# A linear-attention and channel-mix kernel on one core: a new written-out table of instruction order, the last tile's two parts exchanged, and one vector loaded by one DMA

## The chip, the core and the metric

The kernel runs on one core of a Trainium2 chip. The metric is the device time in microseconds of one launch. The five engines go by their short names: PE (TensorE, the matmuls; PEld is the loading of its weights), ACT (ScalarE), DVE (VectorE), POOL (GpSimd, which here does little beyond issuing the casting loads) and SP (SyncE, which issues the stores and the DMA transposes).

## The reference, cut to what matters

There are 8 batches, 8 heads, 576 tokens, a head dimension of 64, a model width of 512 and a hidden width of 1024.

```python
kv  = np.einsum('bhsd,bhse->bhde', k, v)            # 64 x 64 for each head
out = np.einsum('bhsd,bhde->bhse', q, kv)
x   = out / sqrt(mean(out * out) + 1e-6) * g_norm   # norm over each head's 64 values
# x is then (batch, token, 512); x_prev is x moved down by one token
xk = mu_k * x + (1 - mu_k) * x_prev
xr = mu_r * x + (1 - mu_r) * x_prev
k  = np.maximum(xk @ w_k, 0.0)
v  = k * k @ w_v
return sigmoid(xr @ w_r) * v
```

## The kernel before

All tiles are allotted by hand and the order of all work is written out by hand too: `ORDER` (L18 to L109) is a table of eight strings, and the loop at L806 goes through its words from left to right and calls one small function for each. A word such as `K.2.4.0=7` is an operation's name, its arguments, and the PSUM banks that it takes; a quote mark at the end gives the operation to DVE, otherwise to ACT (where there is a choice). Every engine runs its own instructions in the table's order, and waits only for the data, the banks and the buffers that it needs. Nothing reorders at run time, so an instruction that waits holds up all that stands behind it on its engine.

The words that the text speaks of, with b the batch:

- `ld.n.b` (L195) is a load of batch b that casts to bf16, issued by POOL; n is 0 for k, 1 for v, 2 for q. Tiles are shared: for even b from 2 on, k goes to `sq0`, v to `qT0` and q to `q0`; for odd b they have tiles of their own (`in_k`, `in_v`, `in_q`). Before it issues, POOL does a small copy (`passed`, L194) for each DMA transpose that the table has issued since the last load, and so waits until that transpose has landed.
- `qd.b` (L302) is a DMA transpose of q, issued by SP, for b from 3 on. `yd.b` (L410) is one of the normalised y into `xT`, for b from 4 on. Both stand in SP's queue between the stores of the output.
- `kv.b` (L287, 72 small matmuls) makes k'v. `kvo` and `kvs` copy it out of PSUM and swap its halves. `u.b.part` (L317, 72 small matmuls over the three parts) makes q times that. `sq`, `red`, `nw`, `mul` square, sum, take the root and multiply; for b under 4, `x` and `x0` (L437) turn the result on PE, and `xo`, `x0o` move it to `xT`. For b from 4 on `yd` turns it, and `gx.b.h` multiplies by g_norm in place.
- `wrap.b`, `dif.b`, `sc.b.w.hp` (L603 on ACT, L605 on DVE) and `add.b.w.h` (L620) make xk (w = 0) and xr (w = 1).
- `K.b.fc.h` (L633, four matmuls, for the first batches `Kp`, `Ka`, `Kz`) is one piece of xk @ w_k with its relu (L625 on ACT, L627 on DVE), and `ks.b.fc` (`ksp`) the square (L639 on ACT, L641 on DVE).
- `R.b.t` (L665, four matmuls) is xr @ w_r for 128 tokens with its sigmoid (L668, ACT). `V.b.t.part` (L675, four matmuls each, or `Vq`) is the product with w_v. `fin.b.t` (L688) multiplies the two on DVE and issues two stores from SP; `fip` issues one from SP and `sta` the other one from ACT.
- `L.0` and `L.1` are the last tile of 128 tokens, in two parts of 384 and 128 columns (`last_vv`, L678): eight matmuls each, a multiplication on DVE, and a store from SP and one from ACT.
- `wm` is a number of matmuls on zeros that keep PE busy in the start; `cols` turns the small vectors (mu_k, mu_r, g_norm) into columns.

The eight strings are stages of the pipeline: the third is that of the matmuls K.2, the fourth of K.3, and so on to the eighth with K.7, with the loads and the attention of later batches woven in. PE runs in-order through all of it.

## Time and profile before

| what | value |
|---|---|
| median of the 3 runs (lowest to highest) | 199.93 us (199.44 to 201.73) |
| time of the profiled execution | 199.34 us |
| its span, first to last instruction | 197.5 us |
| granted TensorE clock over the span | 0.994 |
| PE, DVE, ACT, POOL busy | 185.3, 160.5, 131.5, 28.9 us |
| DMA | 32.75 MB, mean 166 GB/s |

The time of the profiled execution is 1.84 us more than its span. PE is busy for 94% of the span. The part of the span in which PE is idle, 12.2 us, is in four places: the wait for the first inputs, short waits all along, one of 1.24 us at 70.87 us, and the last 4.3 us, when the last products are multiplied and stored. A row of a group gives the count of instructions, their busy time and mean duration, and the idle time of the engine just before them with what ended it.

### The profile page before, as it was taken

To read this page: it belongs to the slowest core of one execution; us is meant where nothing else is said; L and a number is where in the kernel's file an instruction comes from. 1 tells how busy PE (TensorE), PEld (TensorE's weight loads), DVE (VectorE), ACT (ScalarE), POOL (GpSimd) and SP (SyncE) were. 2 spreads that over 40 slices of the span, in tenths; PEclk is the share of its full clock that TensorE was granted. 3 is DMA by queue.
4 is the path that set the end of the run, shared out by engine and by line. 5 is a ranking of instruction groups with operands and counts; after the bars stand their busy time and mean duration, and the time that the engine had idled before them with its cause. 6 is when DMAs were issued, how large, how long until landed. Compare 5 with 4: busy or idle time off the path is not lost.

```text
span 197.5 us, 5653 instructions
## 1 busy us (share of the span) xinstructions
PE 185.3 (94%) x2314; PEld 110.0 (56%) x2337; DVE 160.5 (81%) x351; ACT 131.5 (67%) x277; POOL 28.9 (15%) x50
## 2 busy tenths in 40 slices
PE   7699899999999979999999999999999999999991
PEld 2345664565554746567644577665545766654450
DVE  1369989699989987899989998999999695585531
ACT  3465997766947959978784489889835685612420
POOL 7854333020003200113003003000000000000000
PEclk9999999999999999999999999999999999999997
DMA  6999999999999999999999998884916422022865
GB/s 218 214 211 205 194 206 211 204 208 238 189 198 236 161 245 179 240 183 273 195 164 162 165 176 167 177 168 85 176 42 133 110 53 53 0 51 59 186 166 128
DMA packets 42958, 32.75 MB, mean 166 GB/s; under 512 B 23852, under 2 KB 37428, under 8 KB 42932
## 3 DMA queue, kind: packets, MB, share of 16 engines
q0 software_dynamic: 14400, 16.19, 50.7%
q1 hardware_dynamic: 28132, 15.67, 38.3%
q10 hardware_dynamic: 400, 0.52, 1.1%
q8 instruction: 18, 0.29, 0.6%
q14 instruction: 8, 0.07, 0.1%
HBM read 33.56 MB, written 9.44 MB: 218 GB/s over the span
## 4 chain that ended last, share of the span: by engine, by line
PE 76%; DMA 14%; DVE 4%; issue 2%; ACT 1%; POOL 1%; DVEq 0%; POOLq 0%
PE ps_km L633 30%; PE ps_v L675 25%; PE ps_r L665 14%; DMA in_v<-in_v_dram 6%; DMA xT<-yd 4%; DMA q<-in_q_dram 3%; PE ps_u L317 2%; PE ps_kv L287 2%; DVE yd L400 1%; PE ps_x L437 1%; PE ps_v L683 1%; ACT sq__3051 L358 1%; DVE xk__2503 L620 1%; DVE dx__2403 L597 1%; PE ps_qt L331 1%
## 5 line engine op out<-in xcount | busy, mean ns | idle before, releaser
L675 PE MATMUL ps_v<-wv_sb,sqk 128*128 128x512 bf16 x263 | 63.3, 379 | 1.4 <-issue 0.9
L633 PEld LDWEIGHTS <-wk_sb 128*128 128x128 bf16 x480 | 45.7, 98 | 18.3 <-issue 2.0
L675 PEld LDWEIGHTS <-sqk 128*128 128x128 bf16 x280 | 26.5, 98 | 28.6 <-ACT sqk L639 0.2
L665 PE MATMUL ps_r<-wr_sb,xr 128*128 128x512 bf16 x139 | 34.6, 379 | 0.6 <-ACT sq__3051 L358 0.3
L665 PEld LDWEIGHTS <-xr 128*128 128x128 bf16 x144 | 13.9, 98 | 15.3 <-DVE xr L620 0.8
L625 ACT ACTIVATE rt<-ps_km 128x384 bf16<-128x384 f32 (+2 forms) x19 | 9.0, 492 | 3.0 <-PE ps_km L633 1.6
L633 PE MATMUL ps_km<-xk__1455,wk_sb 128*128 128x288 bf16 x64 | 8.8, 286 | 1.2 <-issue 1.2
L633 PE MATMUL ps_km<-xk__2841,wk_sb 128*128 128x288 bf16 x64 | 9.0, 286 | 0.1
L633 PE MATMUL ps_km<-xk__869,wk_sb 128*128 128x192 bf16 (+1 forms) x64 | 8.9, 287 | 0.0
L633 PE MATMUL ps_km<-xk__3378,wk_sb 128*128 128x288 bf16 x64 | 8.8, 286 | 0.0
L633 PE MATMUL ps_km<-xk__2503,wk_sb 128*128 128x288 bf16 x64 | 8.5, 286 | 0.1
L633 PE MATMUL ps_km<-xk__1965,wk_sb 128*128 128x288 bf16 x64 | 8.4, 286 | 0.0
L633 PE MATMUL ps_km<-xk__3218,wk_sb 128*128 128x288 bf16 x64 | 8.3, 286 | 0.0
L260 PE MATMUL ps_warm<-zeros 128*128 128x512 bf16 x21 | 7.2, 464 | 1.2 <-DVE eps L223 1.2
L427 ACT ACTIVATE xT<-xT,cols 128x1152 bf16<-128x1152 bf16 x5 | 6.0, 1245 | 0.5 <-DMA xT<-yd 0.5
L724 PE MATMUL ps_km<-xk__373,wk_sb 128*128 128x320 bf16 x32 | 5.5, 299 | 0.5 <-ACT rs L510 0.4
L427 ACT ACTIVATE xT<-ps_x,cols 128x256 bf16<-128x256 bf16 (+3 forms) x12 | 5.0, 469 | 0.6 <-PE ps_x L437 0.5
L429 DVE TENSOR_SCALAR xT<-ps_x,cols 128x1024 bf16<-128x1024 bf16 (+3 forms) x8 | 3.6, 466 | 1.6 <-PE ps_x L437 1.6
L260 PEld LDWEIGHTS <-zeros 128*128 128x128 bf16 x22 | 2.3, 114 | 4.5 <-issue 2.2
L641 DVE TENSOR_TENSOR sqk<-rt 128x1280 bf16<-128x1280 bf16 (+3 forms) x6 | 4.4, 727 | 0.1
L194 POOL COPY passed<-xT 1x2 bf16<-1x2 bf16 x2 | 0.6, 319 | 26.1 <-DMA xT<-yd 26.1
L724 PEld LDWEIGHTS <-wk_sb 128*128 128x128 bf16 x32 | 2.9, 97 | 2.4 <-issue 1.2
(405 smaller groups left out, 365.4 us busy)
## 6 DMA issues: line engine op xcount, KB each, us to landing
qT<-in_v_dram POOLq DMA_DIRECT2D x3, 576.0 KB, 14.9
sq<-in_k_dram POOLq DMA_DIRECT2D x3, 576.0 KB, 14.7
q<-in_q_dram POOLq DMA_DIRECT2D x3, 576.0 KB, 8.4
in_q<-in_q_dram POOLq DMA_DIRECT2D x3, 576.0 KB, 10.9
in_k<-in_k_dram POOLq DMA_DIRECT2D x3, 576.0 KB, 14.3
in_v<-in_v_dram POOLq DMA_DIRECT2D x3, 576.0 KB, 17.1
wk_sb<-in_moe_w_k_dram POOLq DMA_DIRECT2D x2, 512.0 KB, 9.7
sqk<-in_k_dram SPq DMA_DIRECT2D x1, 576.0 KB
```

The source lines that it names most:

```text
L260: nc.tensor.matmul(ps, zeros[:, :128], zeros, start=True, stop=True)
L287: nc.tensor.matmul(ps[e][half(i), M, :], kb[half(e), 2 * M + i, tok(j)], vb[half(e), 2 * M + i, tok(j)], start=(j == 0), stop=(j == G - 1))
L317: nc.tensor.matmul(out_, qT_[half(r), b // 2, half(ct % 2)], kv_[half(r), 0 if r == i else 1, ct, :], start=True, stop=True)
L331: nc.tensor.transpose(ps[e][half(i), j, :], qb[half(e), 2 * M + i, tok(j)], ident[half(e), half(e)])
L427: eng.activation(out=dst, in_=src, func=AF.Copy, scale=g_sb)
L429: eng.tensor_scalar(out=dst, in0=src, scalar1=g_sb, scalar2=None, op0=ALU.mult)
L625: eng.activation(out=dst, in_=ps, func=AF.Relu)
L633: nc.tensor.matmul(ps[:, n, :], wk_sb[:, cc, 128 * fc:128 * fc + 128], at[b]["xk"][:, cc, c0:c1], start=(cc == 0), stop=(cc == NHP - 1))
L641: eng.tensor_mul(out=sqk[:, fcs, o:o + n], in0=src, in1=src)
L665: nc.tensor.matmul(ps, xr[:, cc, 128 * t:128 * t + 128], wr_sb[:, cc, :], start=(cc == 0), stop=(cc == NHP - 1))
L675: nc.tensor.matmul(ps, sqk[:, fc, 128 * t:128 * t + 128], wv_sb[:, fc, :], start=(fc == 0), stop=(fc == NFC - 1))
L724: nc.tensor.matmul(ps[:, n, :], wk_sb[:, cc, 128 * fc:128 * fc + 128], at[0]["xk"][:, cc, c0:c1], start=(cc == 0), stop=(cc == NHP - 1))
```

## The change

Three things change.

The table is replaced as a whole. It has the same words: no operation is added or dropped, and all sizes stay. What differs is where each stands, which banks it takes, and for a good hundred words whether DVE or ACT does it. The last two words of the table are exchanged, so that the wide part of the last tile (384 columns) comes before the narrow one (128). And g_norm, which was written to its two places by two DMAs of 256 bytes, comes by one that reads it twice.

The diff, with the lines of the table that the text speaks of (the table in full is twice 90 lines):

```diff
     """
...
-    fin.1.5 dif.2 sc.2.0.3 sc.2.0.0' V.1.4.1 sc.2.0.2' V.1.6.0=2 V.1.8.0=5 sc.2.0.1 V.1.6.1 ld.0.5 add.2.0.1
-    sc.2.1.2 V.1.7.1 V.1.8.1 add.2.0.0 kvs.3.1 ld.1.5 sc.2.1.1 fin.1.6 sc.2.1.3
...
+    Kp.1.1.5=3 mul.2.0.1 mul.2.1.0 mul.2.0.0 ksp.1.1.4.6 V.1.5.0=6 kv.3=10 mul.2.1.1 ld.1.5 ld.1.4 kvo.3.0
+    mul.2.2.0 ksp.1.0.0.8' qd.3 ld.0.4 x.2.0.4=73 x0.2=25 V.1.6.0=4 x0o.2.0' V.1.6.1 V.1.5.1 x0o.2.1' V.1.7.0=1
+    kvo.3.1 ld.0.5 xo.2.0.4.1 xo.2.0.4.0' V.1.7.1 wrap.2 dif.2 sc.2.0.0 V.1.4.0=0 fin.1.6 sc.2.0.1 sc.2.0.2
+    V.1.4.1 kvs.3.1 kvs.3.0' sc.2.1.3 sc.2.1.1 sc.2.0.3' u.3.1=25 sq.3.1.0 fin.1.5 sq.3.1.1 add.2.0.0 fin.1.7
+    add.2.0.1 u.3.0=37 sq.3.0.1 fin.1.4 sc.2.1.0' u.3.2=4
     """,
     """
-    K.2.4.0=7 u.3.0=46 fin.1.4 qd.4 u.3.2=1 fin.1.7 u.3.1=23 sq.3.0.0 kv.4=07 sq.3.0.1 fin.1.8 add.2.1.1
...
+    K.2.7.1'=6 sq.3.2.0 K.2.4.0'=1 sq.3.0.0 K.2.4.1=0 K.2.1.0=6 add.2.1.0 K.2.2.1=1 red.3.5.9 K.2.6.0=0
...
+    K.2.3.0=0 R.2.1=6 mul.3.1.0 mul.3.1.1 K.2.3.1=1 ks.2.0 V.1.8.0=3 mul.3.0.1 kv.4=02 x.3.0.4=65 mul.3.2.0
...
     """
-    K.6.7.1=0 fin.5.4 K.6.1.1'=6 K.6.0.1=4 add.6.1.0 K.6.4.1=3 K.6.5.1=0 V.5.7.1 gx.7.0' gx.7.1 wrap.7 K.6.5.0=6
...
+    K.6.2.0'=1 K.6.7.0=5 K.6.0.0=3 sc.6.1.3 fin.5.8 K.6.0.1=1 K.6.3.0=5 add.6.1.0 K.6.7.1=7 sc.6.1.2 add.6.1.1
...
-    V.7.6.1 fip.7.7 fin.7.4 R.7.8=0 fip.7.6 sta.7.6 sta.7.7 L.1=2 L.0=7
...
+    fin.6.3 fin.7.4 R.7.8=1 V.7.5.0=5 V.7.5.1 fip.7.7 fip.7.5 sta.7.7 sta.7.5 L.0=3 L.1=0
     """,
 )
...
-    for e in range(2):
-        nc.sync.dma_start(out=rows[8:9, 64 * e:64 * e + 64], in_=g_norm.rearrange("(o p) -> o p", o=1))
+    nc.sync.dma_start(out=rows[8:9, :].rearrange("o (e p) -> o e p", e=2),
+                      in_=g_norm.rearrange("(o p) -> o p", o=1).unsqueeze(1).to_broadcast([1, 2, HD]))
```

## The prediction

> **What bounds the kernel now.** I read the page first, then the busy time by stage, then the chain that ended last.

> ```profile
> span 197.5 us, 5653 instructions
> PE 185.3 (94%) x2314; PEld 110.0 (56%) x2337; DVE 160.5 (81%) x351; ACT 131.5 (67%) x277; POOL 28.9 (15%) x50
> PE 76%; DMA 14%; DVE 4%; issue 2%; ACT 1%; POOL 1%; DVEq 0%; POOLq 0%
> ```

> ```profile
> core 0: us, PE busy (x) PEld busy (x) DVE busy (x) ACT busy (x) POOL busy (x), PEclk, DMA share, GB/s
> 15.00:64.60 49.60, 47.85 (x743) 28.04 (x748) 45.80 (x103) 36.98 (x82) 10.95 (x16) 1.00 1.19 208
> 64.60:86.00 21.40, 19.71 (x423) 12.88 (x425) 19.00 (x40) 17.89 (x42) 2.40 (x4) 1.00 1.24 209
> 86.00:111.90 25.90, 25.45 (x281) 14.73 (x283) 24.37 (x53) 19.45 (x40) 3.31 (x6) 1.00 1.12 192
> 111.90:152.00 40.10, 39.39 (x436) 24.23 (x441) 38.16 (x83) 30.24 (x64) 1.51 (x3) 1.00 0.83 144
> 152.00:193.20 41.20, 40.95 (x250) 24.31 (x252) 26.30 (x53) 19.24 (x38) 0.00 (x0) 1.00 0.36 84
> 193.20:197.50 4.30, 0.00 (x0) 0.00 (x0) 0.56 (x1) 0.00 (x0) 0.00 (x0) 0.75 0.47 118
> ```

> PE ends the chain for three quarters of the span, and from 15 to 193 us it stands still for only 4.9 us (the windows less their busy time). No order of the same matmuls gains more there. The DVE column is what I worry about: from 15 to 152 us it is idle for 3.8 + 2.4 + 1.5 + 1.9 = 9.6 us of 137, so it is a second bound close behind PE. After 152 us it has 15 us of air.

> PE's one long wait is in the 64.6 to 86 stage:

> ```profile
> 65.56 0.76 PE ps_u L317 x66
> 66.32 0.81 PE ps_kv L287 x72
> 67.13 3.74 PE ps_km L633 x29
> 70.87 1.24 issue
> 72.11 1.03 PE ps_km L633 x7
> ```

> ```profile
> q8 instruction: 18, 0.29, 0.6%
> ```

> "Issue" says that no data were late. What stands ahead of it is u.3 and kv.4 side by side: 144 small matmuls, each with a weight load, so 288 instructions in 1.6 us. The queue of instruction code brought 0.29 MB in 18 packets, 16 KB each, and PE and PEld together have 4651 instructions, 258 for each packet. I read the wait as a block of code that was not there yet: 256 instructions around here are gone through in some 5.1 us (counting on from 65.8 to 70.9 us), the quickest block of the kernel after the start.

> **The change part by part.**

> The set of words is the same, so no engine gets or loses an operation, apart from the choice of DVE or ACT. What counts is what stands ahead of what. I counted the PE words and the durations on DVE along both tables.

> (a) The code wait. In the new table u.3 stands ahead of all of K.2, and kv.4 behind its 16 pieces, R.2.1 and half of V.1.8: some 9.5 us of PE work lie between. Counted in blocks of 256, the quickest block of the new table is 5.5 us (kv.7 to behind u.7), the next 5.7. All are longer than the 5.1 that stalled. So the 1.24 us go; at worst another block takes the wait over (0).

> [...]

> (b) The tail.

> ```profile
> 192.14 0.29 DVE L688 TENSOR_TENSOR out__3704<-ps_v,sig__3688 128x128 f32<-128x128 f32 x1 [0.81 <-ACT sig__3688 L668]
> 193.20 0.56 DVE L688 TENSOR_TENSOR out__3717<-ps_v,sig__3688 128x384 f32<-128x384 f32 x1 [0.77 <-PE ps_v L683]
> 194.03 0.56 ACTq L698 DMA_DIRECT2D out_dram<-out__3717  x1
> 191.41 1.76 PE ps_v L683 x16
> out_dram<-out__3717 SPq DMA_DIRECT2D x1, 96.0 KB, 2.1
> out_dram<-out__3704 ACTq DMA_DIRECT2D x1, 32.0 KB, 1.9
> ```

> Now the last store is issued by ACT at 194.03, 2.62 us after the last tile's first matmul, and a wide store lands 2.1 us after its issue: 4.7. With the wide part first, its matmuls end about 1.3 us after the start, its multiplication (0.56) runs beside the narrow matmuls, the narrow multiplication (0.29) ends at about 2.2, and ACT issues the wide store at 1.9 and the narrow one at 2.5; it lands 1.9 later: 4.4. Gain 0.3 us, between 0 (ACT's queue one issue later) and 0.6.

> (c) g_norm by one DMA: one issue of 0.3 us less on SP, which then has nothing to issue until 43 us. Nothing waits for it: 0.

> (d) The start. Until 15 us the landing of the inputs and of w_k sets PE's first real work, and their issues are not moved. 0, between -0.5 and +0.5.

> (e) DVE. Here the new table costs. Take the point where K.6 starts:

> ```profile
> 151.10 0.75 DVE L620 TENSOR_TENSOR xk__3218<-m__3186,xT 128x1152 bf16<-128x1152 bf16 x1
> 152.26 2.61 PE L633 MATMUL ps_km<-xk__3218,wk_sb 128*128 128x288 bf16 x20
> 154.88 0.86 PE ps_v L675 x4
> L627 DVE TENSOR_SCALAR rt__3454<-ps_km 128x288 bf16<-128x288 f32 x2 | 0.9, 457 | 2.8 <-PE ps_km L633 2.8
> L641 DVE TENSOR_TENSOR sqk<-rt__2106 x1: 451/451/451, 95.8 to 95.8; 128x576 bf16<-128x576 bf16 x1
> L605 DVE TENSOR_SCALAR m__901<-dx__822,cols 128x576 bf16<-128x576 bf16 x4 | 1.4, 362 | 0.0
> ```

> The last sum for xk of batch 6 ends at 151.85 and K.6's first matmul starts at 152.26: 0.4 us of slack. Ahead of that sum the new table puts on DVE 20 relus and takes away 11, net +4.4 us by rows like the one shown (the early ones are wider); squares +10 and -6, +1.9; copies and moves out of PSUM +19 and -11, +1.9; scales +7 and -21, -5.2. Net +3.0 us. And PE reaches K.6 with two half-products less behind it (three V words stand behind K.6 that stood ahead, one the other way): 2 x 0.86 = 1.7 us sooner, work that still has to follow. Without any gain elsewhere PE would end 3.0 + 1.7 - 0.4 = 4.3 us later. Ahead of K.2 the same count gives +3.3 us on DVE and PE 1.0 us sooner, so the debt is made in the first third and carried.

> Against that stands DVE's idle time, as far as it has a named cause:

> ```profile
> DVE xT L429 <- PE ps_x L437: 1.6, 2, 1.3
> DVE xk__869 L620 <- ACT m__842 L603: 1.0, 1, 1.0
> DVE qT__440 L218 <- PE ps_qt L331: 0.6, 1, 0.6
> DVE xk__1965 L620 <- ACT m__1874 L603: 0.5, 1, 0.5
> DVE xT L429 <- DMA xT<-yd: 0.5, 1, 0.5
> DVE yd L400 <- DMA xT<-yd: 0.4, 1, 0.4
> ```

> These are the six longest of the 12 in the list from 15 to 152 us; the other six, of 0.2 to 0.4, are two for PE and four for ACT. By cause it is 2.8 us for PE, 0.9 for DMA, 2.5 for ACT, 6.2 in all; the rest of the 9.6 is in the small gaps between instructions, and stays. When DVE is the late one, its waits for PE go, since PE then waits for it (2.8). The two for a transpose go as well, because yd.4 stands 5 us of PE work earlier in the new table (0.9). Of the waits for ACT I count 1.0 as saved, since ACT is the engine that gets the 14 scales. That is 4.7 us recovered, so DVE sets K.6 at 4.3 - 4.7 = -0.4 us. The bounds are 4.3 (nothing recovered) and -1.9 (all 6.2).

> (f) DMAs. Loads and transposes are moved most. The one that is tightest:

> ```profile
> 43.26 1.18 SPq L698 DMA_DIRECT2D out_dram<-out__1027  x2
> 46.75 10.14 SPq L302 DMA_TRANSPOSE qT__1115<-in_q  x1
> 62.22 0.23 POOL L194 COPY passed<-qT__1115 1x2 bf16<-1x2 bf16 x1 [18.40 <-DMA qT__1115<-in_q]
> qT__2634<-in_q SPq DMA_TRANSPOSE x1, 4.7
> q<-in_q_dram POOLq DMA_DIRECT2D x3, 576.0 KB, 8.4
> sq<-in_k_dram POOLq DMA_DIRECT2D x3, 576.0 KB, 14.7
> ```

> qd.3 landed 15.5 us after its issue, beside four loads. SP issues it behind the four stores of the first products, of which fin.0.3 (the first row) now stands 7.5 us of DVE work later: I put qd.3 at about 51.6, 4.9 later. u.3 needs it, and comes about 2.5 us sooner, at 63. In the new table only one load is then in flight, since ld.0.4 and ld.1.4 are put behind; between the 4.7 us of the transpose that had the queues to itself and 15.5 I take 8.5, so it lands at 60 and u.3 does not wait. Bounds: 0 and 51.6 + 15.5 - 63 = 4.1 us. Behind it ld.0.4 waits on POOL for qd.3, until some 61, and kv.4 needs it at some 73: room for 12 us, between the 8.4 of a load with few beside it and the 14.7 of this tile's loads in full queues; nearer the first here. The other transposes have 1 to 3 us of room by the same kind of count, much as before. 0.

> **The sum.** PE alone would give -1.24 (a) and -0.3 (b), and PE's idle time in the stage before K.4, 0.45 in the windows, is a wait for DVE's last sums that could go (-0.4): -1.9. But DVE allows only -0.4 at K.6, which is the later one and so counts, and behind it comes the tail's -0.3: -0.7 us. 199.34 - 0.7 = 198.6 for an execution like the profiled one. That was 0.10 under the lowest and 0.59 under the median of the runs shown; I add the middle of the two, 0.35: **199.0 us**.

> **The rivals.**

> 1. DVE does not set K.6, because all of the 6.2 us are recovered: PE's own sum of -1.9 to -2.3 (with (d) at -0.5) holds. 199.34 - 2.1 + 0.35 = 197.6. For it: DVE's waits vanish where it is behind. Against: all of ACT's 2.5 us would have to go too.

> 2. Slower: DVE recovers little. It decides from 2.3 us recovered downwards: 4.3 - 2.0 - 0.3 = +2.0, 201.7, and with 1 us 202.7. The place is the wait of K.2's first matmul for add.2.0.1, and again K.4 and K.6. For it: 92 to 95% busy is already high, and the new table loads ACT too, so adds may wait for scales. Against: 2.8 us of the idle time are waits for PE, which a late DVE cannot have.

> 3. Slower by a late transpose: qd.3 takes over 11.4 us again and u.3 waits, up to 4.1 us: 203 at the end. Against it speaks that the queues are emptier.

> [...]

> **How the numbers follow.** Forecast 0.45 (198 to 200.6), rival 1 0.20, rival 2 0.20, rival 3 0.10, rival 4 0.05. The range goes from rival 1's lower half to rival 2 and most of rival 3: 197.2 to 203.0. Within 1% of 199.93 (197.9 to 201.9; 1% is about what a measurement of this kernel tells from no change) lie the forecast, rival 4 and small shares of the others: 0.50. Faster by more: most of rival 1 and a little of the forecast, 0.24. Slower by more: 0.26 from rivals 2 and 3.

> **What would show it.** Right: no wait of PE over 0.5 us for "issue" between 60 and 80 us; DVE busy for over 47.5 us of the stage that ends at K.2; the waits of DVE for PE ps_x and ps_v gone; K.2 or K.6 waiting for L620 by up to 1.5 us; the last narrow store landing about 4.4 us after the last tile's first matmul. Wrong: PE waiting for the transposed q at u.3, or for loads at kv.4 or kv.6; a new code wait beside kv.7 and u.7; a start in which PE gets to kvh.0 more than 0.5 us later.

## The result and the profile after

The changed kernel takes 198.96 us (median of 12 runs, 197.91 to 199.86) beside 199.87 us for the kernel before (12 runs, 199.39 to 201.73): a ratio of 0.9939, interval 0.9913 to 0.9965. In a second series it was 198.71 us (11 runs) beside 200.24 (22 runs): 0.9918, interval 0.9888 to 0.9948. The forecast was 199.0.

The page of the profiled execution (199.79 us, so not one of its quicker ones):

```profile
span 198.0 us, 5657 instructions
PE 186.9 (94%) x2313; PEld 110.6 (56%) x2337; DVE 160.8 (81%) x355; ACT 135.7 (69%) x273; POOL 28.1 (14%) x50
PEclk9999879999999999999999999999999999999999
PE 69%; DMA 18%; DVE 5%; issue 3%; ACT 2%; POOL 1%; DVEq 0%; POOLq 0%
```

The span is longer than the 197.5 us of before, although the median of the runs is lower. The clock row tells why: it dips in the fifth and sixth slice. The busy time by stage, with the dip in a stage of its own:

```profile
core 0: us, PE busy (x) PEld busy (x) DVE busy (x) ACT busy (x) POOL busy (x), PEclk, DMA share, GB/s
15.00:22.90 7.90, 6.10 (x108) 3.78 (x108) 7.38 (x20) 5.20 (x13) 3.31 (x5) 1.00 1.17 199
22.90:26.60 3.70, 3.70 (x36) 2.68 (x36) 2.62 (x5) 2.17 (x7) 1.07 (x2) 0.56 1.22 205
...
66.40:86.00 19.60, 19.23 (x293) 12.28 (x289) 19.05 (x40) 17.27 (x39) 2.91 (x4) 1.00 1.21 224
86.00:112.20 26.20, 25.46 (x348) 15.01 (x350) 25.03 (x56) 20.23 (x41) 1.09 (x3) 1.00 1.16 178
112.20:151.20 39.00, 38.45 (x437) 23.67 (x441) 36.95 (x80) 31.36 (x64) 2.58 (x5) 1.00 0.75 141
151.20:192.10 40.90, 40.64 (x241) 23.95 (x245) 24.22 (x49) 22.17 (x43) 0.00 (x0) 1.00 0.39 89
```

From 22.9 to 26.6 us PE ran at 0.56 of its clock: 1.6 us lost. In the stage of K.2 it now stands still for 0.4 us instead of 1.7, and the chain of waits has nothing between u.3 and the end of the sixty matmuls of K.2, where before stood 1.24 us of issue:

```profile
65.70 0.80 PE ps_u L317 x72
66.50 7.57 PE ps_km L633 x60
```

At the end ACT issues the wide and the narrow store of the last tile, whose first matmul started at 192.28 (the chain's time), and the narrow one lands 2.2 us behind its issue:

```profile
194.27 0.50 ACTq L698 DMA_DIRECT2D out_dram<-out__3703  x1
194.86 0.78 ACTq L698 DMA_DIRECT2D out_dram<-out__3716  x1
```

Sorted by the granted clock, the 23 runs of both series fall in two groups: 8 with 0.992 or less (median 199.37) and 15 above (198.22). So the forecast number stands between the medians of two groups, and the experiments have to tell what makes each.

### The profile page after: what moved, and what is told of

The parts are those of the page before. It is cut to its first block, busy times and chain, and to the rows that moved or that the text cites. A ratio compares the mean times of both kernels' runs of the same rounds, so it can differ in the third digit from the quotient of the medians.

```text
span 198.0 us, 5657 instructions
## 1 busy us (share of the span) xinstructions
PE 186.9 (94%) x2313; PEld 110.6 (56%) x2337; DVE 160.8 (81%) x355; ACT 135.7 (69%) x273; POOL 28.1 (14%) x50
## 4 chain that ended last, share of the span: by engine, by line
PE 69%; DMA 18%; DVE 5%; issue 3%; ACT 2%; POOL 1%; DVEq 0%; POOLq 0%
PE ps_km L633 26%; PE ps_v L675 24%; PE ps_r L665 13%; DMA sq<-in_k_dram 6%; DMA in_q<-in_q_dram 6%; DMA q<-in_q_dram 3%; DMA xT<-yd 3%; PE ps_kv L287 2%; PE ps_u L317 1%; PE ps_x L437 1%; DVE yd L400 1%; PE ps_qt L331 1%; DVE xr L620 1%; PE ps_u L542 1%; PE ps_v L683 1%
## 5 line engine op out<-in xcount | busy, mean ns | idle before, releaser
L675 PE MATMUL ps_v<-wv_sb,sqk 128*128 128x512 bf16 x264 | 64.4, 379 | 1.4 <-issue 1.0
L633 PEld LDWEIGHTS <-wk_sb 128*128 128x128 bf16 x480 | 46.6, 100 | 17.8
L675 PEld LDWEIGHTS <-sqk 128*128 128x128 bf16 x280 | 26.6, 98 | 28.3 <-issue 0.2
L625 ACT ACTIVATE rt<-ps_km 128x320 bf16<-128x320 f32 (+2 forms) x17 | 7.9, 490 | 6.6 <-PE ps_km L633 4.8
L260 PE MATMUL ps_warm<-zeros 128*128 128x512 bf16 x21 | 8.2, 523 | 1.2 <-DVE eps L223 1.2
L633 PE MATMUL ps_km<-xk__871,wk_sb 128*128 128x192 bf16 (+1 forms) x64 | 9.2, 286 | 0.0
L633 PE MATMUL ps_km<-xk__3378,wk_sb 128*128 128x288 bf16 x64 | 9.0, 286 | 0.0
L633 PE MATMUL ps_km<-xk__1956,wk_sb 128*128 128x288 bf16 x64 | 8.7, 286 | 0.0
L633 PE MATMUL ps_km<-xk__2733,wk_sb 128*128 128x288 bf16 x64 | 8.7, 286 | 0.0
L633 PE MATMUL ps_km<-xk__2399,wk_sb 128*128 128x288 bf16 x64 | 8.7, 286 | 0.0
L633 PE MATMUL ps_km<-xk__3224,wk_sb 128*128 128x288 bf16 x64 | 8.7, 286 | 0.0
L633 PE MATMUL ps_km<-xk__1498,wk_sb 128*128 128x288 bf16 x64 | 8.3, 286 | 0.0
L633 PE MATMUL ps_km<-xk__371,wk_sb 128*128 128x256 bf16 x32 | 5.5, 345 | 0.0
L195 POOL DMA_DIRECT2D in_v<-in_v_dram x3 | 2.2, 748 | 21.2 <-PE ps_kv L287 17.2
L641 DVE TENSOR_TENSOR sqk<-rt 128x768 bf16<-128x768 bf16 (+3 forms) x7 | 4.9, 703 | 0.1
L427 ACT ACTIVATE xT<-xT,cols 128x1152 bf16<-128x1152 bf16 x4 | 5.0, 1294 | 0.0
L603 ACT ACTIVATE m__2392<-dx__2382,cols 128x576 bf16<-128x576 bf16 x4 | 2.9, 765 | 3.1 <-DVE dx__2382 L597 3.1
## 6 DMA issues: line engine op xcount, KB each, us to landing
q<-in_q_dram POOLq DMA_DIRECT2D x3, 576.0 KB, 14.5
sq<-in_k_dram POOLq DMA_DIRECT2D x3, 576.0 KB, 14.6
qT<-in_v_dram POOLq DMA_DIRECT2D x3, 576.0 KB, 9.9
in_v<-in_v_dram POOLq DMA_DIRECT2D x3, 576.0 KB, 13.7
in_q<-in_q_dram POOLq DMA_DIRECT2D x3, 576.0 KB, 9.8
in_k<-in_k_dram POOLq DMA_DIRECT2D x3, 576.0 KB, 17.4
sqk<-in_k_dram SPq DMA_DIRECT2D x1, 576.0 KB, 3.9
```

Of the source, the lines that this page charges most:

```text
L195: nc.gpsimd.dma_start(out=x_in[name, b], in_=by_token(dram[name], b))
L260: nc.tensor.matmul(ps, zeros[:, :128], zeros, start=True, stop=True)
L427: eng.activation(out=dst, in_=src, func=AF.Copy, scale=g_sb)
L603: eng.activation(out=out_, in_=in_, func=AF.Copy, scale=mu)
L625: eng.activation(out=dst, in_=ps, func=AF.Relu)
L633: nc.tensor.matmul(ps[:, n, :], wk_sb[:, cc, 128 * fc:128 * fc + 128], at[b]["xk"][:, cc, c0:c1], start=(cc == 0), stop=(cc == NHP - 1))
```

## The experiments

### Is the wait of 1.24 us a late block of code?

The theory of the prediction was that PE waits for a block of 256 instructions. The rival is that the wait belongs to that place in the order. To tell them apart, the order of the kernel before was left alone, and its code was moved, by 192 and by 64 instructions:

```diff
     warm(12)
+    def small(n):
+        ps = take("small", [128, 64], FP32, "ps_small")
+        for i in range(n):
+            nc.tensor.matmul(ps[half(i % 2), :], zeros[half(i % 2), :64], zeros[half(i % 2), :64], start=True, stop=True)
+        give("small")
+    small(96)      # 32 in the second kernel
```

> The kernel before, its order untouched, with 96 matmuls of 64 x 64 on zeros (192 instructions with their weight loads) behind the warm-up matmuls, where PE waits for its first input anyway. Nothing reads them; they only move every later instruction of PE 192 places on in the code, so that a block of 256 that was missing at instruction 2235 would now be wanted at 2043 (in kv.4, called for a good 256 instructions earlier, at about 60 us) and the next at 2299 (75 us). Theory of the code wait: the 1.24 us of issue at 70.87 us are gone, and the time falls by about 1.2 us, to 198.7, less what the fillers cost in the start (0 to 0.5). Rival (the wait belongs to that place in the order, not to the code): 1.2 us of issue stay inside K.2.1.0, and the time is 199.9 or more.

Measured: 204.05 us, ratio 1.0182 (1.0141 to 1.0224). The wait at 70.87 us is gone, as expected, but the time did not fall. PE's waits, the longest first:

```profile
PE ps_ms L506 <- issue: 2.8, 1, 2.8
```

A new one of 2.8 us stands at 9 us in the start, behind a stretch in which 205 of PE's instructions take 1.9 us (7 to 9 us), and the clock is 0.50 from 10.9 to 17.7 us. The wait moved with the code. That it would come up again at that place was not foreseen.

> As the run with 96, with 32 such matmuls (64 instructions). The block is now wanted at instruction 2171, where K.2 goes on after kv.4 (67.0 us), and called for between 65.0 and 65.7 us. With the 6 us that the block took in the kernel before (called for at about 66, used at 72.1) the theory of the code wait has PE stand still at 67.0 us for 3.5 to 4.8 us, and the time rises by 2.5 to 3.5 us, to 202.4 to 203.4. Rival (not the code): the 1.24 us stay at K.2.1.0, 199.9.

Measured: 211.82 us, ratio 1.0594 (1.0546 to 1.0642). PE's waits, and the counts of its instructions between the ends of the three long ones (47.60, 74.47 and 132.39 us; columns as in the stage table above):

```profile
PE ps_r L665 <- issue: 3.6, 1, 3.6
PE ps_kv L287 <- issue: 3.5, 1, 3.5
PE ps_qt L331 <- issue: 1.8, 1, 1.8
```

```profile
47.60:74.47 26.87, 23.33 (x384) 12.40 (x384) 22.48 (x42) 16.39 (x30) 3.14 (x5) 0.94 1.12 205
74.47:132.39 57.92, 54.35 (x767) 33.98 (x767) 50.79 (x109) 43.35 (x97) 5.93 (x11) 0.97 1.02 179
71.00:74.40 3.40, 0.00 (x0) 0.00 (x0) 2.24 (x4) 0.13 (x1) 0.00 (x0) 1.00 1.18 234
74.50:78.00 3.50, 3.50 (x19) 2.31 (x20) 0.00 (x0) 2.56 (x8) 0.00 (x0) 0.58 1.18 232
```

384 + 384 is 768, three times 256; 767 + 767 is 1534, two records short of six times 256. The waits stand on a raster of 256 instructions. The one of 3.5 us is where the theory put it, within a few instructions of the end of kv.4, and as long as it said (3.5 to 4.8). The two others, and the half clock behind each wait (0.52, 0.58 and 0.60 over the next 3.4 to 3.5 us), had not been counted. The three waits are 8.9 us where the kernel before has 1.24, and three times 3.4 us at half clock cost up to 1.7 us each: that covers the 12 us.

The 256 of the prediction was an estimate from 18 packets of 16 KB and 258 instructions for each; the counts above show it. In the profiles of the kernel before and of the changed one, each of the first 13 stretches of 256 from a count of 193 on has one such packet, begun 0.1 to 4.1 us after the stretch's first instruction (a few records are missing there). When a block is called for stands in no view: the times for it in the expectations of these two runs are estimates. In these runs a late block costs up to 3.6 us. In the seven waits of over 1 us on the raster in the profiles that keep all of PE's records, the packet of code ends 1.2 to 1.5 us before PE goes on, and 3.6 to 5.2 us after the block before was begun.

### Is the new order safe from it?

> The changed kernel with the five fillers and 80 matmuls of 64 x 64 on zeros (160 instructions) behind the warm-up ones, read by nothing: the code of everything behind moves by 160 places. In the five profiles so far that keep all of PE's records, every long wait for issue on PE stands at a count of 193 + 256 n instructions (matmuls and weight loads), the 16 KB packet of code ends 1.2 to 1.5 us before the wait does, and it ends 2 to 5.5 us after the block before was begun. So a block that PE goes through in less than some 3.5 us (DMA queues half empty) to 6.2 us (full) costs the difference. Theory: with this shift the quick blocks of the changed order are the one around 10.5 us (wait of 2.0 to 2.6 us at a count of 449) and the one that ends at 58.5 us (0.5 to 1.0 at 1985), the clock may drop behind the first, and the time is 200.5 to 202.5. Rival (the order with its dense stretches set apart is proof against code waits, wherever the blocks fall): 198.0 to 198.4.

Measured: 202.08 us, ratio 1.0069 (1.0036 to 1.0102). PE's waits, and the stage behind the first:

```profile
PE ps_kv L474 <- issue: 1.7, 1, 1.7
PE ps_kv L287 <- DMA sq<-in_k_dram: 1.2, 1, 1.2
```

```profile
13.50:17.00 3.50, 3.50 (x35) 1.59 (x37) 2.08 (x6) 1.28 (x3) 1.43 (x2) 0.56 1.14 209
```

The wait at a count of 449 came, 1.7 us instead of 2.0 to 2.6, with a drop of the clock behind it; the one at 1985 did not. So the new order is free of code waits only where its blocks happen to fall now: the same order with 160 more instructions ahead is slower than the kernel before.

### What drops the clock?

After each of the five code waits of 1.7 to 3.6 us above, PE ran for some 3.4 us (once 6.8) at about half its clock; after the 1.24 us of the kernel before it stayed at 1.00. In the changed kernel the longest wait of PE between 15 us and the drop is 0.63 us, but the stretch ahead of the drop is thin (columns as above; the changed kernel, then the one before):

```profile
19.00:22.90 3.90, 2.52 (x85) 1.52 (x84) 3.62 (x10) 3.62 (x10) 1.88 (x3) 1.00 1.17 194
```

```profile
19.00:22.90 3.90, 3.20 (x105) 1.96 (x102) 3.76 (x11) 3.43 (x9) 2.21 (x3) 1.00 1.18 193
```

PE is idle for 1.38 us of 3.9 there instead of 0.70. The first kernel fills these gaps:

```diff
-    Kz.0.6 sc.0.1.3' qt.1.0=26
+    Kz.0.6 sc.0.1.3' wm.2.8=2 qt.1.0=26
-    Kz.0.3 kvh.0=17 kvho.0.0 kvho.0.1' uh.2.0=0
+    Kz.0.3 wm.2.9=1 kvh.0=17 kvho.0.0 kvho.0.1' wm.1.9=0 uh.2.0=0
```

> The changed kernel with five matmuls on zeros (0.22 us each at full clock) in the three places around 20 to 23 us where PE waits (0.44 us for in_q, 0.63 us for in_v, 0.31 us for the copy of kv): two, two and one. They have no reader. Theory: the half clock that the changed kernel's profile shows from 22.9 to 26.6 us follows from PE's low activity just before it (1.38 us idle of 20 to 23 us, small matmuls in the rest), so with the gaps filled no dip comes, in no execution: granted clock 0.998 or more in all, and a time near that of the changed kernel's undipped executions, 198.0 to 198.4, 0.9% below the kernel before. Rival: the dip comes from elsewhere (the whole load of the stage, chance); then half of the executions still show a clock of about 0.990 and the median stays at 199.0. If the fillers delay the first attention of batch 1 instead, K.2 starts up to 1 us later at a clock of 1.0.

Measured: 197.99 us, ratio 0.9908 (0.9877 to 0.9940). The stretch is 3.54 us busy, and the clock row of its profile is flat:

```profile
19.00:22.90 3.90, 3.54 (x87) 1.86 (x85) 3.71 (x10) 3.56 (x10) 1.92 (x3) 1.00 1.19 194
```

```profile
PEclk9999999999999999999999999999999999999999
```

One of its six executions still dropped (clock 0.989, 198.90 us), so "in no execution" was too much.

> The changed kernel once more, unchanged, beside a kernel with the fillers on the same chip, to see how often its clock drops. Theory (low activity of PE at 20 to 23 us lets the clock drop): a clock of 0.992 or less in a third to a half of its executions, as in 5 of 12 before, and those 1.0 to 1.5 us longer than the others; its undisturbed executions 198.0 to 198.4. Rival (the first sample was chance): as rare as in the kernel before, 1 in 8.

Measured: 198.71 us; three of 11 executions at 0.991 or less, 199.14, 199.29 and 201.17, the others 197.42 to 199.14. Its profile has a drop as well, but at 10 to 13 us, behind a wait of 1.5 us for the copy of the first inputs, and its stretch of 19 to 22.9 us, which came later against the transfers, is 3.46 us busy.

Together, with 0.992 or less: the changed kernel 8 of 23 executions, the kernels with fillers 3 of 42 (this one and three below; those with moved code or a transpose that came late are left aside), the kernel before 14 of 85. The drop is thus no property of the change. That it is rarer with the fillers is hardly chance: 3 of 42 beside 8 of 23 would come up about once in 80 if both dropped equally often (the chips differ, but the kernel before dropped about as often on them: 8 of 52 on those of the fillers, 3 of 22 on that of the second series). That the change made it more frequent is not shown: 8 of 23 beside 14 of 85 would come up about once in 13, and of the two profiles of the changed kernel only one has the thin stretch at 19 us.

What decides from one execution to the next can be read from the clock records of the 14 profiles. Ahead of the last matmuls each stretch of half clock is 3.41 us long, or two or three times that, and all switches of one execution stand on one raster of 3.41 us, whose place differs from profile to profile. Cut along this raster, the traces hold 775 pieces at full clock. Behind all 16 in which PE is busy for less than 1.9 us (8 of them at the end, where the matmuls run out) the next piece is at half clock; behind none of the 752 with more than 2.1 us is it; of the 7 between, one has half clock behind it. That one is in the changed kernel's profile, and it and its successor are (columns as above):

```profile
19.94:23.35 3.41, 2.03 (x96) 1.33 (x94) 3.23 (x8) 2.68 (x8) 1.71 (x3) 1.00 1.17 192
23.35:26.76 3.41, 3.41 (x26) 2.42 (x19) 2.33 (x6) 2.17 (x7) 0.74 (x1) 0.50 1.21 205
```

Between 3 and 190 us of that profile a piece has under 2.1 us only if it starts from 19.4 to 20.2 us. If the place of the raster is random, it falls there in about a quarter of the executions (0.8 of 3.41 us), an estimate beside the measured 8 of 23. In the profile with the five fillers alone no piece between 15 and 190 us would have under 2.7 us, wherever the raster stands. No profile caught a drop of the kernel before, so where those lie is open.

### The tail, and g_norm by one DMA

```diff
-    ... sta.7.7 L.1=2 L.0=7
+    ... sta.7.7 L.0=7 L.1=2
```

> The kernel before with only the last two words exchanged (wide part of the last tile first). The prediction's term (b): -0.3 us (0 to -0.6), the last store landing 4.4 us after the last tile's first matmul instead of 4.7, the stretch from that matmul to the end of the span 5.7 to 5.8 us instead of 6.1. Rival: the end is set by the wide store's own chain and the exchange gives nothing (6.1 us stays).

Measured: 200.11 us, ratio 1.0003 (0.9977 to 1.0029). ACT's stores of the last tile, whose first matmul is at 191.66 in the chain, and the landing of the last:

```profile
193.64 0.50 ACTq L698 DMA_DIRECT2D out_dram<-out__3704  x1
194.24 0.79 ACTq L698 DMA_DIRECT2D out_dram<-out__3717  x1
```

```profile
out_dram<-out__3717 ACTq DMA_DIRECT2D x1, 32.0 KB, 2.2
```

The issues come at 1.98 and 2.58 us, as worked out in the prediction. But the narrow store lands 2.2 us behind its issue, not 1.9: 4.8 in all, where the kernel before has 2.62 + 2.1 to 2.2. From the first instruction of L683 to the last packet it is 4.50 us instead of 4.61. The exchange is worth 0.1 us.

In the changed kernel, however, the span ends 5.90 us after that instruction, and in these two after 6.28 and 6.25. The difference is behind the last packet: 1.67 us before, 1.76 here, 1.40 in the changed kernel. The DMAs take eight semaphores in turn, and at the end SP waits for all eight in a fixed order (in the trace 108, 110, 112, 114 to 118).

> The kernel before with the last two words exchanged and g_norm by one DMA, that is, all of the change but the table. In the run with the words alone exchanged, SP goes through eight closing waits (0.063 us each) after the last store has landed, because that store carries the semaphore that stands first in SP's closing list; eight semaphores go round over the DMAs in turn. One DMA fewer at the start shifts the turn by one, so that the last store carries the one that stands last in the list. Theory: from the last store's last packet to the end of the span 1.35 to 1.40 us instead of 1.76, as in the changed kernel, so 0.4 us less in all, about 199.6 where the words alone gave 200.0. Rival (the prediction's term (c)): nothing, 1.76 stays. In the start PE may wait 0.3 us for the one DMA (it takes longer to issue than each of the two), hidden behind the wait for the copies of k and v.

Measured: 199.55 us, ratio 0.9977 (0.9949 to 1.0005). SP's semaphore instructions from the last packet on, in the kernel with the exchange alone and in the one with g_norm by one DMA as well (a group's line: count, duration, first and last start):

```profile
L836 SPq EVENT_SEMAPHORE  x10: 17/28/28, 196.4 to 197.7; - x10
```

```profile
L836 SPq EVENT_SEMAPHORE  x5: 17/28/28, 196.5 to 197.7; - x5
```

Five waits fewer, and 1.27 us from the last packet to the end instead of 1.76. The changed kernel and its variants have 1.35 to 1.40, all kernels with two DMAs 1.67 to 1.76. So the one DMA does pay, 0.3 to 0.5 us, but at the other end of the kernel: it changes which store carries the semaphore that stands first in SP's list. In the trace the last store carries 108, the first, in the kernels with two DMAs; 118, the last, in this one; and 117 in the changed kernel. The whole time shows it less clearly: the intervals of the two ratios overlap, and the two profiled spans are 197.8 and 197.7 us, because in the second PE waited 0.5 us for ACT at 88 us.

### Does DVE set K.6?

```diff
-    K.5.7.1=2    K.5.2.1=4    K.5.1.1=4    K.5.0.0=4
+    K.5.7.1'=2   K.5.2.1'=4   K.5.1.1'=4   K.5.0.0'=4
```

> The changed kernel with the five filler matmuls, and four relus of K.5 (K.5.7.1, K.5.2.1, K.5.1.1, K.5.0.0) put from ACT to DVE: 4 x 0.457 = 1.8 us more on DVE in the 25 us ahead of K.6. In the run with the fillers alone the last sum for xk of batch 6 ends at 150.01, K.6 starts at 149.9 to 150.1, and the durations on DVE up to that sum add up to 149.64. Theory (the prediction's term (e): DVE sets K.6 and has nothing left to recover): K.6 starts 1.4 to 1.8 us later and the time rises to 199.4 to 199.8, with PE waiting for L620 at K.6. Rival (PE alone is the bound, the sum of durations hides overlaps and DVE has room): less than 0.5 us, 198.0 to 198.4.

Measured: 200.42 us, ratio 1.0015 (0.9985 to 1.0046), where the fillers alone have 0.9908. First matmuls of K.4 and of K.6, and the two last sums for xk of batch 6, with the fillers alone and then with the four relus on DVE:

```profile
110.83 0.91 PE L633 MATMUL ps_km<-xk__2407,wk_sb 128*128 128x288 bf16 x6
148.59 1.42 DVE L620 TENSOR_TENSOR xk__3232<-m__3202,xT 128x1152 bf16<-128x1152 bf16 x2
150.13 1.88 PE L633 MATMUL ps_km<-xk__3232,wk_sb 128*128 128x288 bf16 x14
```

```profile
110.58 1.15 PE L633 MATMUL ps_km<-xk__2407,wk_sb 128*128 128x288 bf16 x8
149.75 1.42 DVE L620 TENSOR_TENSOR xk__3232<-m__3202,xT 128x1152 bf16<-128x1152 bf16 x2
151.28 0.78 PE L633 MATMUL ps_km<-xk__3232,wk_sb 128*128 128x288 bf16 x5
```

From K.4 to K.6 it takes 40.70 us instead of 39.30: 1.4 of the 1.8 us arrive, as the theory of the second bound has it. K.6 starts 0.1 us behind the last sum in both. The median rose further than the 199.4 to 199.8 us expected; the profiled execution, with 199.65 one of the quicker, does not show by what.

```diff
-    K.5.2.0'=7   K.5.6.1'=5   K.5.3.0'=2   K.4.3.1'=7
+    K.5.2.0=7    K.5.6.1=5    K.5.3.0=2    K.4.3.1=7
```

> As the kernel with the fillers, with four relus (K.5.2.0, K.5.6.1, K.5.3.0, K.4.3.1) put from DVE to ACT: 1.8 us less on DVE ahead of K.6. Theory of DVE as the bound up to K.6: PE can come forward only by the idle time that it still has between 111 and 150 us, 0.14 us, and by what it waited for DVE before; at most 0.3 us, 197.7 to 198.0, and the last sum ends 1 to 1.8 us ahead of K.6 instead of with it. Theory that DVE held PE back all along through late PSUM banks: up to 1 us, 197.0. If ACT (32.2 of 39.1 us busy there) becomes the late one: up to 0.5 us slower.

Measured: 199.25 us, ratio 0.9957 (0.9932 to 0.9982), beside 0.9908 (0.9877 to 0.9940) with the fillers alone: probably slower, though the intervals touch. K.6 starts at 151.37 instead of 150.13. What came was the case named last, a little larger: ACT is late.

```profile
PE ps_r L665 <- ACT rt__2893 L625: 0.8, 1, 0.8
```

So the split of the relus between the two engines is tight: in both profiles a move of four, in either direction, brings K.6 more than 1 us later. Whether DVE held PE back all along, by up to 1 us, this run cannot tell, because the four relus made ACT late.

### The loads of batches 4 and 6

In the profile with the fillers the longest wait of PE behind 40 us is for a load of k:

```profile
PE ps_kv L287 <- DMA sq<-in_k_dram: 0.6, 1, 0.6
```

```diff
-    K.3.5.0=4 ld.0.6 fin.2.3
+    K.3.5.0=4 fin.2.3
-    R.2.3=1 qd.5 K.3.3.1'=0
+    R.2.3=1 qd.5 ld.0.6 K.3.3.1'=0
```

> As the kernel with the fillers, with the load of k of batch 6 (ld.0.6) right behind the transpose qd.5 in the table instead of behind yd.4. POOL then waits for qd.5 alone (landed at 96.3 in the changed kernel) and not for yd.4 (99.05): the load is issued 2 to 3 us sooner, and the 0.6 us that PE waits for it at kv.6 should go. If PE is the bound there and DVE is not, the gain reaches the end: -0.6, 197.4. If DVE sets K.6 (theory), PE is 0.6 sooner at kv.6 but waits for the sum at K.6: the time stays within 0.2 of 198.0. A risk for both: yd.4 (5.1 us) runs beside the load, lands 2 to 3 us later and its readers wait.

Measured: 198.29 us, ratio 0.9918 (0.9888 to 0.9947), the same as with the fillers alone within the intervals. It decides nothing: in the kernel with the fillers the wait was at kv.4, not at kv.6 as in the changed kernel's own profile (its ld.0.6 landed in time), and here kv.4 waited for 1.5 us. The load to move was ld.0.4:

```diff
-    red.2.0.5 R.1.8=3 ... kv.3=10 mul.2.1.1 ld.1.5 ld.1.4 kvo.3.0 ... qd.3 ld.0.4
+    red.2.0.5 ld.0.4 ld.1.4 R.1.8=3 ... kv.3=10 mul.2.1.1 ld.1.5 kvo.3.0 ... qd.3
```

> The changed kernel with the five fillers, and with the loads of k and v of batch 4 (ld.0.4, ld.1.4) 7 us sooner in the table, ahead of ld.1.5 for which POOL waits until kv.3 is through (58.9). In the changed kernel ld.0.4 is issued at 60.86 behind it and lands at 75.54, and kv.4 wants it at 75 to 76: PE waited for it by 0.6 us in the run with the fillers and by 1.5 in another. Theory: the load lands by 70, the wait goes, and PE is 0.6 to 1.0 sooner at K.4; at the end 0.3 to 0.6 of it are left where DVE allows (197.5 to 197.7 where the fillers gave 198.0). Rival 1: DVE, which has 3 us of idle time left at K.4 and 0.4 at K.6, takes all of it back at K.6: 0. Rival 2: the transpose qd.3 (51.8 to 59.4), with four loads beside it, takes over 12 us and u.3 waits: slower by 0.5 to 2.

Measured: 204.95 us, ratio 1.0248 (1.0215 to 1.0281): the second rival, and more. The loads were issued at 46.4 and 47.1 us; the transpose qd.3 and the u.3 that reads it:

```profile
50.57 10.95 SPq L302 DMA_TRANSPOSE qT__1367<-in_q  x1
69.59 1.28 PE L317 MATMUL ps_u<-kv__1286,qT__1367 64*64 64x64 bf16 x72 [5.13 <-DMA qT__1367<-in_q]
```

The transpose took 19.0 us. In the changed kernel, issued at 51.81 with one load in flight, it took 7.6.

```diff
-    kv.3=10 mul.2.1.1 ld.1.5 ld.1.4 kvo.3.0 ... qd.3 ld.0.4
+    kv.3=10 mul.2.1.1 kvo.3.0 ... qd.3 ld.0.4 ld.1.4 ld.1.5
```

> The changed kernel with the five fillers and the three loads that POOL issues around 59 to 61 us in another order, all of them behind the transpose qd.3: ld.0.4, which is wanted first (kv.4 at 75 us), then ld.1.4, ld.1.5, instead of ld.1.5, ld.1.4, ld.0.4. In the run with the fillers ld.0.4 is issued at 59.90, third of the three, and lands at 75.62, and PE waits 0.6 us for it. Theory: issued at about 59.0, first of the three, it lands by 72 and the wait goes. What becomes of the 0.6 us tells who sets K.6: if PE does, K.6 starts at 149.3 and the end is 0.6 sooner (197.4 where the fillers gave 198.0); if DVE does (0.4 us of idle time left there), K.6 starts at 149.6 to 149.9 and the time stays at 197.7 to 198.0. Rival: the load is slowed by the others all the same and lands after 75: nothing changes.

Measured: six executions at 198.85, 203.96 and four from 208.32 to 209.05 us. The load did what the theory said, it landed at 68.5 and kv.4 did not wait. But the four loads now start 3.2 to 5.4 us ahead of the next transpose, qd.4, instead of 7.2 to 9.5 in the changed kernel. In the profile, which is of the slowest execution:

```profile
67.00 12.50 SPq L302 DMA_TRANSPOSE qT__1848<-q  x1
90.61 1.28 PE L317 MATMUL ps_u<-kv__1707,qT__1848 64*64 64x64 bf16 x72 [9.01 <-DMA qT__1848<-q]
```

It took 23.6 us and u.4 waited for 9.0; in the changed kernel it took 13.2. Who would take back the 0.6 us at K.6 is left open by this run.

The lowest time of the study is that of the changed kernel with five filler matmuls, 197.99 us, ratio 0.9908; its interval overlaps those of the changed kernel (0.9939 and 0.9918).

## Why the prediction was right, and where it was not

**The number** is right, 199.0 against 198.96, the sum only in part. Executions without a clock drop are at 198.22, against 200.08 for such executions of the kernel before in the later series: between the forecast's 198.6 to 199.0 and rival 1. Those with it are at 199.37. Terms too small on one side and a loss not foreseen on the other made up for each other, and that the number is hit so closely is luck. The profiles do not account for all of it either: the span is 196.7 us with the fillers and 197.5 before, of which 0.4 us are gained ahead of the last tile and 0.4 behind it; the other 1.0 us between 200.08 and 198.22 stays open.

**(a) The code wait**: right in its cause, since the wait moved with the code and three waits stood whole multiples of 256 instructions apart. PE has no wait for issue over 0.2 us behind 40 us in the profiles of the changed kernel and of the one with the fillers. The size was -1.24; a second profile of the old table, the one with the tail exchanged, has 1.7 us (1.5 at this place, 0.2 at 88 us), and a third 1.8. The reasoning that 5.5 us a block are enough and 5.1 are not was too simple: on the true raster the quickest block of the new order takes 4.4 us (with the fillers, up to 135 us, with kv.7 and u.7) and does not wait: the packet of the next one came 1.8 us after it was begun, with a DMA share of 0.75 in that stage. In the full queues of 66 to 86 us (1.21) the packet takes 4.8.

**(b) The tail** was mis-sized: -0.1 instead of -0.3. The issues were right to 0.1 us, the landing of a narrow store was taken from one that did not come last.

**(c) g_norm** was costed at nothing because nothing waits for it. Wrong: -0.3 to -0.5, through the turn of the semaphores at the end. Tail and g_norm together give -0.4, near the -0.3 that (b) alone was to give.

**(d) The start** was looked at up to 15 us only, and put at 0 with half a microsecond either way; no term has the clock. This is the step that failed. Around the small matmuls at 20 to 23 us the old table has six of K.0's matmuls and the new one two, PE's idle time at 19 to 22.9 us is 1.38 us instead of 0.70 in one profile of the changed kernel (0.44 in the other, which drops earlier), and kvh.0 starts at 22.09 and 22.51 instead of 21.68. The clock drops in about a third of the executions, beside a sixth before; a drop costs 1.15 us (199.37 against 198.22).

**(e) DVE** came out right in the net, by two errors that cancelled. Up to the last sum for K.6 the durations of DVE's instructions add up to 147.6 us before and 150.7 with the fillers: +3.1, forecast +3.0. But neighbouring instructions overlap, and the time in which DVE is busy grew by only 0.5 us, from 127.18 to 127.70 (columns as in the stage table; before, then with the fillers):

```profile
15.00:151.85 136.85, 132.25 (x1879) 79.79 (x1896) 127.18 (x276) 104.56 (x226) 18.18 (x28) 1.00 1.08 187
```

```profile
15.00:150.01 135.01, 133.25 (x1894) 79.59 (x1895) 127.70 (x282) 104.44 (x215) 17.49 (x28) 1.00 1.05 185
```

Its idle time fell from 9.7 to 7.3 us: 2.4 recovered, forecast 4.7. The waits for transposes went (0.9), and 1.4 us of those for ACT, but the waits for PE did not: 3.1 us instead of 2.8. The forecast took its cost from durations and its gain from idle time, and each is over 2 us too large: 0.5 - 2.4 = -1.9, forecast 3.0 - 4.7 = -1.7. K.6 starts at 150.13 instead of 152.26, with 1.7 us of PE's work moved behind it: a gain of 0.4, as forecast; and the last tile's first matmul is 0.4 sooner too (191.01 against 191.41 in the chains). Rival 2's late K.6 did not come, although hardly more idle time was recovered than the 2.3 us from which it was to decide. Two of the signs named for DVE as the bound failed: PE does not wait for L620 at K.2 or K.6, it arrives as the sum is ready, and DVE's busy time in the stage up to K.2 is 46.9 us with the fillers, not over 47.5. The third held in part: DVE's waits for ps_x are gone, of ps_v one of 0.2 us is left. The run with four more relus on DVE still shows DVE as the bound at K.6.

**(f) The DMAs**: qd.3 was issued at 51.81 (forecast 51.6) and took 7.6 us (8.5); u.3 did not wait. Rival 3 was real, but needs the loads ahead of the transpose; the two runs with other loads show 19.0 and 23.6 us. For ld.0.4 the wrong end was taken: it took 14.7 us, not something near 8.4, and landed at 75.5, just ahead of kv.4 at 76.3. In other profiles kv.4 waits for it, 0.6 to 1.5 us. The 0 of this term has no room left in it.

**Rival 4** (0.05) is that the code wait stays. With the wait left in, PE's sum is -0.7 and DVE's -0.4 at K.6 still counts: 199.34 - 0.7 + 0.35 = 199.0 again. So the time alone does not tell it from the forecast; the profiles do, in which the wait is gone.

## What to carry to other kernels

A wait of PE for issue inside a dense stretch is worth a count: here such waits were whole multiples of 256 instructions apart and moved with the code, and 64 instructions on zeros added ahead made 211.8 us of 199.9, so the place of the blocks is to be measured again after each edit. Behind each of the 16 pieces of 3.41 us with PE busy for less than 1.9 us stood a half clock; with five matmuls on zeros in the gaps 3 of 42 executions had a drop, without them 8 of 23. Durations of DVE's neighbouring instructions overlapped here (+3.1 us added up, +0.5 us of busy time), so a cost added up from durations and a gain read from idle time do not belong in one sum. And loads belong behind a DMA transpose that is wanted soon: here two attempts to save 0.6 us by bringing a load forward made a transpose late by 5 and by 9 us.
